# Moving the scale of phi(K) onto V, converting score tiles in pairs, and building the identity's ramp in PSUM, in a gated mix of linear and softmax attention

## The chip, the core and the metric

The kernel runs on one core of a Trainium2 chip. The time is what the device takes for one execution, in microseconds; the median of three runs stands for a kernel. Five engines work side by side, each on its own list of instructions in order: PE (matrix products into PSUM), ACT (activation functions such as exp), DVE (elementwise work and reductions), POOL (elementwise work on SBUF) and SP, which here only issues transfers. They wait for each other through semaphores. PSUM has eight banks of 512 fp32 words in each of 128 partitions.

## The reference

Two attention layers over the same x (2048 rows, 512 columns, 32 heads of 16), mixed by a gate; the inputs are bf16. A is linear attention with a softmax feature map, B is softmax attention.

```
g = sigmoid((x * gate_w).sum(-1))
# A
q, k, v = split(x @ A_wqkv)                       # 32 heads of 16
phi(t)  = concat[softmax(t @ w_phi), softmax(-(t @ w_phi))]    # 32 features a head
kv = einsum("bhsf,bhsd->bhfd", phi(k), v);  z = sum over s of phi(k)
a  = (phi(q) @ kv) / (phi(q) @ z + 1e-6)  @ A_wo
# B
b  = softmax(q k^T / 4) v @ B_wo                  # 2048 x 2048 scores for each head
out = g * a + (1 - g) * b
```

## The kernel before

**Softmax attention is the bulk.** The scores are cut into 2048 tiles of 128 keys x 512 queries: 32 blocks (a chunk of 512 queries, and one of the heads of each group of four), each with 4 heads x 16 key tiles. A tile is named (b, i, kt). The scores of one tile are one matrix product (`qk_mm`, L819) into one PSUM bank. Its exponential can be made in two ways:

- **By ACT.** Two tiles at a time fill two banks and one `activation` of 1024 columns writes their exponentials (`add_exp`, L898 to L901). Such a pair is a slot; slots alternate between the banks S0, S1 and S2, S3. The exponentials go to a ring of 12 places (`Ebuf`), and `add_pv` multiplies them by V (`pv_mm`, L917 to L922; four heads stand side by side in the columns of PE and add into the one bank psO).
- **By DVE and POOL.** DVE turns one tile of scores into int16 words whose bits, read as bf16, approximate the exponential (`tensor_scalar`, L889). POOL then adds two constants to the words of a group of up to four tiles (`shifted`, L864 to L871, one `int64_add` for each constant), which gives the same values with shifted mantissas, and PE multiplies all three versions by V (`add_pvd`). `DN` (L31) says how many tiles of each of the 32 blocks go this way. They sum to 684 before and 694 after; the other tiles, two by two, make 682 slots before and 677 after.

Scores for DVE, and all the other products of the program, share three banks: psM and the fifth and sixth bank of psS (`MISC`, L503). `fill` (L584) gives a product such a bank, `drain` (L606) is the instruction that empties it and sets it free.

**Linear attention fills the gaps.** For each of 16 row tiles `st`, `phi(1, ...)` (L1161) projects x by a weight that already holds w_phi; ACT takes exp of it and of its negative (`both`, L1169) into `EA`, which has two places; DVE sums each head's 16 features (L1177). For every second tile DVE inverts the sums (L1193) and multiplies the features by them (`scaled`, L1203) into `phiK`. `va_fill` (L1154) projects V, and DVE copies it to `vA`, with a column of ones beside each group of four heads. After eight row tiles `kv_half` (L1217) multiplies `phiK` by `vA`: 128 features (two signs x four heads x 16) by 65 columns, summed over the eight tiles; `kfinal` masks the result to the blocks on the diagonal. Then the same is done for Q (`phi(0, ...)`), whose features go through DRAM to be transposed (`q_write`, `q_turn`), multiplied by K's result (`q_rest`, L1265), and again through DRAM (`o_turn`).

**The start.** The first 512 rows of x come in as they lie (transfers of L513) and PE transposes them by means of an identity matrix. DVE builds the identity (L549 to L553): a ramp 0..31 in every partition by doubling (one memset, five additions), its 32x32 transpose `quad`, and four comparisons of the two. From `quad` come `pmask` and `half2`, masks for even and odd heads. Meanwhile PE runs seven products to warm up (L540), POOL clears tiles and issues a few transfers. The first projections and the first scores follow the transposes of x.

**The order of all work** is made by a planner in the kernel's source (`Plan.layout`, L161): it simulates the engines with assumed durations and at each step takes the ready operation with the lowest priority number. The numbers at the top of the file (L31 to L68) are priorities, paces and paddings of this plan. `K_AT + K_PACE * st` and `Q_AT + Q_PACE * i` are the priorities of the row tiles of K and Q, `KG_AT` to `QG_PACE` the slot from which they may begin, `OP_AT` and `O_AT` those of the output projections, `D_FIRST` the slot after which VectorE tiles begin. The engines then run their lists in that fixed order. On PE the scores of the slots come first, and when nothing is ready it multiplies zeros (`zero_mm`, L910 to L912). The flag `lock` marks DVE operations that the plan doesn't put beside one of POOL.

Four output tiles end the program. Two of them (`SPLIT`) are made in two parts, the larger one beforehand (`out_part`, L1102, evicted at L1107), and two by `out_last` (L1111, evicted by ACT at L1119).

Of the kernel before, what the change touches and what calls it, by code (L numbers as in the profile page):

```python
# [9 lines left out]
F32 = mybir.dt.float32  # L10
# [20 lines left out]
DN = (8, 20, 18, 22, 26, 22, 22, 20, 20, 18, 20, 18, 22, 22, 22, 22, 22, 22, 22, 26, 26, 20, 22, 26, 18, 26, 24, 18, 18, 20, 32, 20)  # L31
# [4 lines left out]
STICK = 56.1  # L36
UNITS = 564.8
W_AT = 21.402
D_FIRST = 14
# [6 lines left out]
T_PRIO = 31.922  # L46
DQ_PRIO, DQ_K = 6.035, 1.527
KG_AT, KG_PACE, QG_AT, QG_PACE = 48.282, 10.47, 269.933, 10.468
R1_AT, R1_PACE, R2_AT, R2_PACE, R3_AT, R3_PACE = 34.139, 13.552, 132.978, 16.57, 282.947, 5.294
TR_LAT, TR_ISSUE = 3.0, 0.4  # L50
OP_AT, OP_PACE = 686.29, 4.0
SPLIT = (14, 15)
O_AT, O_PACE = 514.821, 11.487
# [3 lines left out]
QK_TOL = (0.374, 0.192)  # L57
TURN_PAD = 2.257
G_DEEP = 6
K_AT, K_PACE, Q_AT, Q_PACE = 74.787, 10.55, 262.62, 10.076  # L60
POOL_ADDS = (0, 203, 69, 203, 69, 203, 69, 195, 69, 235, 69, 203, 69, 195, 69, 202, 69, 218, 69, 203, 101, 203, 68, 195, 69, 219, 65, 203, 71, 203, 69, 203)
SHIFT = (0.25, 3.63, -8.78, -3.32, -9.03, -1.63, -2.79, 0.92, 2.51, 6.48, 3.43, 8.42, 1.31, -1.12, -3.56, -1.52, 5.83, 8.06, 0.55, 2.18, 3.47, 1.77, 2.23, -4.16, -0.22, 0.96, 4.59, -6.01, -4.6, -0.62, -4.99, 2.66)
P64, W64 = 0.19, 0.21
M_LATE = -15.682
D_AHEAD = 23.328
CONT = -58.411
# [12 lines left out]
class Op:  # L79
    __slots__ = ("eng", "dur", "prio", "fn", "deps", "succ", "nd", "ready", "end", "lat", "sem", "count",  # L80
                 "name", "full", "extra", "room", "fill", "bank_of", "acq", "rel", "seq", "clock", "take", "pos", "margin", "done", "kind", "heads", "lock", "cols", "alive", "semval", "pad")

    def __init__(self, eng, dur, prio, fn, name):
# [10 lines left out]
        self.pad = 0.0  # L94
        self.kind, self.heads, self.lock = None, (), False
# [13 lines left out]
class Bank:  # L109
    def __init__(self, name, ap):  # L110
        self.name, self.ap = name, ap
        self.free, self.shared = True, True
        self.last, self.until = [], 0.0


class Plan:
# [43 lines left out]

    def layout(self):  # L161
        for op in self.ops:
            op.nd = len(op.deps)
            for d in op.deps:
                d.succ.append(op)
# [15 lines left out]
        while left:  # L181
# [30 lines left out]
            for e in ENGINES:  # L212
# [11 lines left out]
                if e == "pe" and last_pe is not None and busy[e] > t - 1e-6:  # L224
                    want = {"qk": "dq", "dq": "dq"}.get(last_pe, "term")
                    for item in sorted(queues[e]):
                        o = item[2]
                        if o.kind == want and not used_heads & set(o.heads) and o.ready <= pe_start + RIDE_TOL and (
                                o.kind == "dq" or o.prio < T_PRIO or active >= ACTIVE[3]):
                            if o.acq is not None:  # L230
# [4 lines left out]
                                o.acq.bank = min(bs, key=lambda b: max([0.0] + [x.end for x in b.last]))  # L235
# [21 lines left out]
                while queues[e] and pick is None:  # L257
# [5 lines left out]
                    elif op.lock and max(lock_end[o] for o in lock_end if o != e) > t + 1e-9:  # L263
                        pass
                    elif op.take is not None:
                        if all(b.free for b in op.take):
                            pick = op
                    elif op.acq is not None:
                        bs = [b for b in op.acq.banks if b.free and b.shared and b.until <= t + 1e-9]
                        if bs:  # L270
                            op.acq.bank = min(bs, key=lambda b: max([0.0] + [o.end for o in b.last]))
                            pick = op
# [29 lines left out]
                op = pick  # L302
                if e == "pe":
# [43 lines left out]
                heapq.heappush(finish, (op.end, op.seq, 1, op))  # L347
                heapq.heappush(events, op.end)
# [5 lines left out]
    def emit(self, block, sems):  # L354
        counts = {e: 0 for e in ENGINES}
# [71 lines left out]
def _build(ctx, nc, A_x, A_wqkv, A_w_phi, A_wo, B_wqkv, B_wo, gate_w, out):  # L427
# [22 lines left out]
    vAf = sb([128, NT * 8 * 65], name="vA")  # L450
    vA = vAf[:].rearrange("p (a b c) -> p a b c", a=NT, b=8)
# [22 lines left out]
    kv_sb = sb([128, 8, 65], F32, name="kv")  # L474
# [4 lines left out]
    ramp = sb([128, 32], name="ramp")  # L479
    quad = sb([128, 32], name="quad")  # L480
    half2 = sb([128, 2], name="half")
    mask64 = sb([128, 64], name="mask64")
# [9 lines left out]
    psS = ctx.enter_context(nc.psum_tensor("psS", [128, 3072], F32))  # L492
    psO = ctx.enter_context(nc.psum_tensor("psO", [128, 512], F32))
    psM = ctx.enter_context(nc.psum_tensor("psM", [128, 512], F32))
    bS = [Bank(f"S{i}", psS[:, 512 * i:512 * (i + 1)]) for i in range(6)]
    bO = Bank("O", psO[:])
    bM = Bank("M", psM[:])
# [39 lines left out]
    def warm_fn(e):  # L537
        ins = None
        for _ in range(7):
            ins = e.matmul(psM[:], lhsT=Ebuf[:, 0, 0:128], rhs=Ebuf[:, 0, 0:512], start=True, stop=True)  # L540
        return ins
# [6 lines left out]
    small = lambda fn, reads, writes, name, prio=-9.5: P.add("dve", 0.16, prio, fn, reads=reads, writes=writes, name=name)  # L548
    small(lambda e: e.memset(ramp[:, 0:1], 0.0), (), ["ramp"], "r0")  # L549
    for n in (1, 2, 4, 8, 16):  # L550
        small(lambda e, n=n: e.tensor_single_scalar(ramp[:, n:2 * n], ramp[:, 0:n], float(n), ALU.add), ["ramp"], ["ramp"], f"r{n}")  # L551
    small(lambda e: e.transpose(quad[:], ramp[:]), ["ramp"], ["quad"], "quad")
    P.join_writes([small(lambda e, q=q: e.tensor_tensor(ident[32 * q:32 * q + 32, 32 * q:32 * q + 32], ramp[32 * q:32 * q + 32, :],  # L553
                                                        quad[32 * q:32 * q + 32, :], ALU.is_equal), ["ramp", "quad", "id"], [], f"id{q}")
                   for q in range(4)], "ident")
    P.join_writes([small(lambda e, n=n: e.tensor_scalar(pmask[:, n:n + 1], quad[:, 0:1], 16.0, QSCALE, op0=(ALU.is_lt, ALU.is_ge)[n],
                                                        op1=ALU.mult), ["quad"], [], f"pm{n}", -9) for n in range(2)], "pmask")
    P.join_writes([small(lambda e, n=n: e.tensor_single_scalar(half2[:, n:n + 1], quad[:, 0:1], 16.0, (ALU.is_lt, ALU.is_ge)[n]), ["quad"], [],
                         f"hh{n}", 0.0) for n in range(2)], "half2")
# [14 lines left out]
    pool(0.4, -3, lambda e: e.memset(vA[:, :, :, 64:65], 1.0), writes=["vA1"], name="vA1")  # L574
# [248 lines left out]
    def add_qk(j):  # L823
# [15 lines left out]
        op.kind, op.heads = "qk", [t[1] for t in ts]  # L839
        if j < 2:  # L840
            op.margin = 0.1
# [35 lines left out]
    def add_group(g):  # L877
        ft, ops, tb = opening(g["t"]), [], bufs[g["t"]][0]
        before = list(dq_ops)
        dq_ops.clear()  # L880
# [560 lines left out]
```

## Time and profile before

| | us |
|---|---|
| median of 3 runs (lowest to highest) | 704.83 (704.63 to 707.05) |
| the profiled execution | 704.55 |
| its span, first to last instruction | 702.5 |
| first exponential of the softmax starts | 13.79 |
| last one ends | 691.56 |

The groups of DVE and POOL that the change touches (line, engine, operation, tiles and shapes, count; busy us, mean ns of one; idle time before and who ended it):

```profile
L1203 DVE TENSOR_TENSOR phiK_t<-EA_t,stat_t 128x1024 bf16<-128x1024 bf16 x16 | 19.9, 1244 | 0.1
L1177 DVE TENSOR_REDUCE stat_t<-EA_t 128x64 f32<-128x1024 bf16 x16 | 19.4, 1210 | 2.3 <-ACT EA_t L1171 2.2
L1193 DVE RECIPROCAL stat_t<-stat_t 128x128 f32<-128x128 f32 x8 | 7.6, 944 | 0.0
L1158 DVE CAST vA_t<-psS 128x512 bf16<-128x512 f32 x11 | 7.5, 683 | 0.0
L551 DVE TENSOR_SCALAR ramp_t<-ramp_t 128x4 bf16<-128x4 bf16 x1 | 5.1, 5143 | 0.0
L1158 DVE CAST vA_t<-psM 128x512 bf16<-128x512 f32 x5 | 3.4, 683 | 0.0
```

Busy times of the engines by stretch (start:end, length, then busy us and count of PE, weight loads, DVE, ACT, POOL; the granted PE clock, the share of DMA, GB/s):

```profile
13.79:50.00 36.21, 35.49 (x385) 13.14 (x384) 23.36 (x40) 35.81 (x39) 9.96 (x13) 1.00 0.41 97
50.00:260.00 210.00, 207.62 (x2139) 64.79 (x2137) 189.44 (x296) 207.09 (x236) 105.99 (x109) 1.00 0.07 16
260.00:460.00 200.00, 195.06 (x2057) 59.90 (x2055) 190.19 (x312) 198.06 (x225) 112.91 (x117) 1.00 0.14 36
460.00:691.60 231.60, 227.22 (x2383) 67.58 (x2376) 205.17 (x383) 227.18 (x252) 127.69 (x130) 0.99 0.26 62
```

A duration is that of one instruction from start to end; instructions of one engine overlap a little, so the step from one start to the next can be shorter. A matrix product's busy time is modelled, and products that stand side by side in PE count each.

### The profile page before, as it was taken

What the parts mean: (1) busy time and instruction counts of PE and PEld (TensorE: products, weight loads), DVE (VectorE), ACT (ScalarE), POOL (GpSimd) and SP (SyncE); (2) the same over time, 40 slices, a digit from 0 to 9 for tenths busy, and PEclk for the clock granted to TensorE, in tenths of its full rate; (3) what the DMA queues carried; (4) which work ended last, traced back from release to release, by engine and by line L of the source; (5) the groups of instructions that cost most, each with busy time, mean ns of one, the idle gap of its engine ahead of it and who ended that gap; (6) DMA issues with size and microseconds to landing.
All of it is one profiled execution on the core that took longest, in us unless ns stands there. A gap on an engine that the chain in (4) does not pass through costs nothing.

```text
span 702.5 us, 17206 instructions
## 1 busy us (share of the span) xinstructions
PE 683.7 (97%) x7083; PEld 214.1 (30%) x7083; DVE 623.3 (89%) x1056; ACT 672.1 (96%) x753; POOL 369.3 (53%) x394
## 2 busy tenths in 40 slices
PE   6999999999999999999999999999999999999999
PEld 3332332333322332233222222332223322332333
DVE  6499879999999699999999999999989999997783
ACT  3999999999999999999999999999999999999994
POOL 7056457555454155553665665645556554455453
PEclk9999999999999999999999999999999999999999
DMA  6600101001000000000013023121321133125121
GB/s 132 161 19 10 26 17 25 11 13 22 10 17 10 9 21 7 26 10 12 20 29 93 10 75 80 27 65 58 70 70 28 43 80 70 48 84 92 49 62 38
DMA packets 67454, 30.72 MB, mean 44 GB/s; under 512 B 52696, under 2 KB 62296, under 8 KB 67376
## 3 DMA queue, kind: packets, MB, share of 16 engines
q1 hardware_dynamic: 66368, 28.95, 17.2%
q8 instruction: 56, 0.92, 0.6%
q10 hardware_dynamic: 576, 0.52, 0.2%
q0 software_dynamic: 432, 0.15, 0.2%
q14 instruction: 22, 0.18, 0.1%
HBM read 7.87 MB, written 8.88 MB: 24 GB/s over the span
## 4 chain that ended last, share of the span: by engine, by line
PE 76%; ACT 17%; DVE 6%; issue 1%
PE psO L922 28%; PE psS L819 25%; ACT E_t L901 16%; PE psS L614 8%; PE psM L614 6%; PE psO L912 4%; ACT EA_t L1171 1%; DVE ramp_t L551 1%; PE psM L819 1%; DVE Tx_t L889 1%; PE psM L684 1%; PE psS L671 1%; DVE Ty_t L889 1%; DVE statq_t L1177 0%; DVE Tf_t L1016 0%
## 5 line engine op out<-in xcount | busy, mean ns | idle before, releaser
L901 ACT ACTIVATE E_t<-psS 128x1024 bf16<-128x1024 f32 x682 | 642.6, 1062 | 11.0 <-PE psS L819 6.0
L819 PE MATMUL psS<-qz_t,kTB_t 32*128 32x512 bf16 x1829 | 275.5, 385 | 9.5 <-ACT E_t L901 7.7
L819 PEld LDWEIGHTS psS<-qz_t,kTB_t 32*128 32x128 bf16 x1829 | 70.0, 91 | 249.1 <-ACT E_t L901 179.7
L889 DVE TENSOR_SCALAR Tx_t<-psS 128x512 int16<-128x512 f32 x181 | 120.6, 681 | 8.6 <-PE psS L819 4.2
L922 PE MATMUL psO<-E_t,vaug_t 128*32 128x512 bf16 x1364 | 113.8, 388 | 0.0
L871 POOL INT64_ADD vA_t<-vA_t x68 | 67.4, 996 | 45.5 <-PE psO L922 28.6
L819 PE MATMUL psM<-qz_t,kTB_t 32*128 32x512 bf16 x219 | 84.3, 385 | 0.0
L871 POOL INT64_ADD Ty_t<-Tx_t x28 | 28.3, 1009 | 54.8 <-DVE Tx_t L889 43.1
L889 DVE TENSOR_SCALAR Ty_t<-psS 128x512 int16<-128x512 f32 x74 | 50.1, 683 | 6.5 <-PE psM L819 3.1
L889 DVE TENSOR_SCALAR Tx_t<-psM 128x512 int16<-128x512 f32 x71 | 48.4, 681 | 4.4 <-PE psS L819 2.9
L871 POOL INT64_ADD Ty_t<-Ty_t x39 | 39.3, 1007 | 17.0 <-PE psO L922 10.6
L922 PE MATMUL psO<-vA_t,vaug_t 128*32 128x512 bf16 x486 | 46.8, 383 | 0.0
L912 PE MATMUL psO<-xT_t,zero_t 128*32 128x512 bf16 x484 | 44.5, 386 | 0.0
L922 PE MATMUL psO<-Ty_t,vaug_t 128*32 128x512 bf16 (+1 forms) x406 | 41.8, 384 | 0.0
L922 PEld LDWEIGHTS psO<-E_t,vaug_t 128*32 128x32 bf16 x1364 | 23.9, 95 | 43.6 <-issue 40.8
L889 DVE TENSOR_SCALAR Ty_t<-psM 128x512 int16<-128x512 f32 x48 | 32.7, 682 | 1.6 <-PE psM L819 1.2
L889 DVE TENSOR_SCALAR oT_t<-psS 128x512 int16<-128x512 f32 x45 | 30.1, 683 | 4.4 <-PE psS L819 3.8
L889 DVE TENSOR_SCALAR Tz_t<-psS 128x512 int16<-128x512 f32 x44 | 29.3, 680 | 2.7 <-PE psS L819 2.6
L889 DVE TENSOR_SCALAR WAT_t<-psS 128x512 int16<-128x512 f32 x43 | 28.8, 679 | 2.8 <-PE psM L819 2.2
L871 POOL INT64_ADD WoA_t<-WoA_t x17 | 16.8, 989 | 26.9 <-PE psO L922 25.2
L871 POOL INT64_ADD phiQT_t<-Tx_t x17 | 16.0, 940 | 27.4 <-DVE Tx_t L889 27.4
L889 DVE TENSOR_SCALAR vA_t<-psS 128x512 int16<-128x512 f32 x42 | 28.3, 679 | 1.0 <-PE psS L819 0.8
(205 smaller groups left out, 1041.7 us busy)
## 6 DMA issues: line engine op xcount, KB each, us to landing
dpq<-EA_t SPq DMA_DIRECT2D x16, 256.0 KB, 2.2
Rb_t<-lr SPq DMA_DIRECT2D x120, 32.0 KB, 1.8
dpo<-kv_t SPq DMA_DIRECT2D x16, 128.0 KB, 1.7
qz_t<-qz_t SPq DMA_DIRECT2D x120, 16.0 KB, 1.8
Tf_t<-Tf_t SPq DMA_DIRECT2D x60, 32.0 KB, 2.0
WB_t<-in_B_wqkv_dram SPq DMA_DIRECT2D x3, 384.0 KB, 4.6
out_dram<-WvA_t SPq DMA_DIRECT2D x8, 128.0 KB, 1.8
out_dram<-WB_t SPq DMA_DIRECT2D x6, 128.0 KB, 1.7
```

The lines of the kernel that those rows point to most:

```text
L551: small(lambda e, n=n: e.tensor_single_scalar(ramp[:, n:2 * n], ramp[:, 0:n], float(n), ALU.add), ["ramp"], ["ramp"], f"r{n}")
L614: return [lambda e, ap, i=i: e.matmul(ap, lhsT=lhs[i], rhs=rhs[i], start=(i == 0), stop=(i == len(lhs) - 1)) for i in range(len(lhs))]
L671: mms = [lambda e, ap, i=i, t=t: e.matmul(ap[:, 128 * i:128 * (i + 1)], lhsT=xT[:, t, NQ * c + 128 * i:NQ * c + 128 * (i + 1)], rhs=W_B[:, ...
L684: mms = [lambda e, ap, i=i, t=t: e.matmul(ap[:, 256 * i:256 * (i + 1)], lhsT=xT[:, t, NQ * c + 128 * (2 * hf + i):NQ * c + 128 * (2 * hf + ...
L819: return e.matmul(bank, lhsT=kT_B[32 * i:32 * i + 32, ROW[b // 2] % 2, 128 * kt:128 * (kt + 1)], rhs=qz[32 * i:32 * i + 32, b // 2 % 4, b ...
L871: op = P.add("pool", P64 + W64 * size, d_prio(g["ts"][0]) - 5.0 + (0.0 if key == "s" else M_LATE), lambda e: e.int64_add(words(dst), words ...
L889: ops.append(drain(f, mm, "dve", 0.70, d_prio(d), lambda e, ap, q=q: e.tensor_scalar(quarter(tb, q).bitcast(I16), ap, EXPB, 0.0, op0=ALU.a ...
L901: op = P.add("act", 0.051 + 0.4267 * n, 0.0, lambda e: e.activation(Ebuf[:, j // 2 % EPAIRS, 512 * SZ[0] * (j % 2):512 * SZ[0] * (j % 2) + ...
L912: ins = e.matmul((psO if bank is None else bank)[32 * i:32 * i + 32, :], lhsT=zero[:], rhs=xT[:, 0, 0:NQ], start=bank is not None, stop=ba ...
L922: return e.matmul(psO[32 * i:32 * i + w, :], lhsT=vaug[:, kt, o:o + w], rhs=rhs, start=start, stop=stop, tile_position=(0, 32 * i), skip_g ...
L1171: ins = e.activation(EA[:, b, :].rearrange("p (g s c) -> p s g c", s=2, c=64)[:, sgn, :, :], ap.rearrange("p (g c) -> p g c", c=64), ACTF. ...
```

## The change

- **Scale of phi(K).** `scaled` is gone: ACT writes the exponentials of K straight into `phiK` and they stay as they are. The reciprocal sums multiply V instead. For each row tile, V is projected after the sums are known and evicted twice, once for each sign, by a DVE product with the sums broadcast over 16 columns; POOL copies the reciprocal sums themselves beside V, where the ones stood. `vA` holds 8 row tiles, two signs each, instead of 16 tiles. The product of `kv_half` is then two products of 64 features (one for each sign) that stand side by side in PE's columns, with 68 columns.
- **Pairs.** psM becomes the seventh bank of psS, so that the three shared banks lie in a row. Where two tiles of the same group are ready for DVE (or one is to be within `PAIR_WAIT`) and lie in neighbouring banks in the same order as in the group, the planner makes one `tensor_scalar` of 2 x 512 columns of them; both banks are freed when it ends. `choose` picks banks so that the order fits.
- **Identity.** The ramp lies in the first columns of psS, in fp32; `quad`, its transpose, in SBUF in fp32; a second transpose, `column`, in PSUM, serves the masks.
- **Numbers.** `DN`, and most of the priorities, paces and paddings of the plan, have other values; `QK_PAD`, `D1_PAIR` and `PAIR_WAIT` are new.

```
-DN = (8, 20, 18, 22, 26, 22, 22, 20, 20, 18, 20, 18, 22, 22, 22, 22, 22, 22, 22, 26, 26, 20, 22, 26, 18, 26, 24, 18, 18, 20, 32, 20)
+DN = (6, 20, 18, 20, 26, 22, 22, 20, 22, 18, 20, 18, 22, 20, 22, 22, 26, 22, 22, 28, 26, 22, 22, 28, 16, 24, 24, 18, 22, 22, 32, 22)
-STICK = 56.1
+STICK = 15.702
-D_FIRST = 14
+D_FIRST = 26
-KG_AT, KG_PACE, QG_AT, QG_PACE = 48.282, 10.47, 269.933, 10.468
+KG_AT, KG_PACE, QG_AT, QG_PACE = 23.892, 7.205, 270.949, 12.608
-OP_AT, OP_PACE = 686.29, 4.0
+OP_AT, OP_PACE = 641.917, 4.0
-K_AT, K_PACE, Q_AT, Q_PACE = 74.787, 10.55, 262.62, 10.076
+K_AT, K_PACE, Q_AT, Q_PACE = 73.65, 11.18, 262.327, 12.484
...
+    def mates(self, a, b):
+        return b.kind == "D1" and a.half[0] == b.half[0] and abs(a.rel.bank.index - b.rel.bank.index) == 1 and (
+            a.half[1] - b.half[1]) * (a.rel.bank.index - b.rel.bank.index) > 0
...
+                    elif op.kind == "D1" and any(r <= t + PAIR_WAIT and self.mates(op, x) for r, _, x in pending["dve"]):
+                        pass
...
+                        op.fn = lambda e, wide=wide, a=(min(q, q2), max(q, q2)), b=(min(b, b2), max(b, b2)): wide(e, a, b)
+                        op.dur = D1_PAIR
+                        op.deps = op.deps + [d for d in other.deps if d not in op.deps]
+                        op.rel = [op.rel.bank, other.rel.bank]
...
+            return e.tensor_scalar(dst[:, a[0]:a[1] + 1:a[1] - a[0], :].bitcast(I16), src[:, b[0]:b[1] + 1:b[1] - b[0], :], EXPB, 0.0,
+                                   op0=ALU.add, op1=ALU.max)
...
-    psM = ctx.enter_context(nc.psum_tensor("psM", [128, 512], F32))
+    psM = psS[:, 3072:3584]
...
-    ramp = sb([128, 32], name="ramp")
-    quad = sb([128, 32], name="quad")
+    quad = sb([128, 32], F32, name="quad")
+    ramp, column = psS[:, 0:32], psS[:, 32:64]
...
-    def va_fill(st, prio):
+    def va_fill(st, prio, after):
...
+        for s in range(2):
+            drain(f, mm, "dve", 0.70, prio, lambda e, ap, s=s: e.tensor_tensor(
+                vA[:, m, :, s, 0:64].rearrange("p g (j d) -> p g j d", j=4), ap.rearrange("p (g j d) -> p g j d", g=8, j=4),
+                by[:, :, s, :].unsqueeze(3).to_broadcast([128, 8, 4, DH]), ALU.mult),
+                reads=[("rs", b), ("ss", b)], writes=[("vA", m, s)], name=f"VAe{st}.{s}", last=s == 1)
+        P.add("pool", 0.3, prio, lambda e: e.tensor_copy(vA[:, m, :, :, 64:68], by), reads=[("rs", b), ("ss", b)],
+              writes=[("vA", m, 2)], name=f"VAr{st}")
...
-    def scaled(qk, st, e3, dst, dkey, prio):
-        b = st % 2
-        phi_ops.append(P.add("dve", 1.22, prio, lambda e: e.tensor_tensor(
-            dst.rearrange("p (g f) -> p g f", f=DH), e3, stat[:, b, :].unsqueeze(2).to_broadcast([128, 64, DH]), ALU.mult),
-            reads=[("EA", b), ("rs", b), ("ss", b)], writes=[dkey], name=f"phi{qk}.{st}"))
-        phi_ops[-1].lock = True
...
+                        for s in range(2):
+                            ins = e.matmul(ap[64 * s:64 * s + 64, 68 * gg:68 * gg + 68], lhsT=phiK[:, m, 128 * g + 64 * s:128 * g + 64 * s + 64],
+                                           rhs=vA[:, m, g, s, :], start=(m == 0), stop=(m == 7), tile_position=(0, 64 * s))
```

159 lines of the change are left out of this document (97 added, 62 removed).

## The prediction

> **What bounds the kernel now.** I read four views. First the page, for the engine that is full.
>
> ```profile
> span 702.5 us, 17206 instructions
> PE 683.7 (97%) x7083; PEld 214.1 (30%) x7083; DVE 623.3 (89%) x1056; ACT 672.1 (96%) x753; POOL 369.3 (53%) x394
> ...
> L901 ACT ACTIVATE E_t<-psS 128x1024 bf16<-128x1024 f32 x682 | 642.6, 1062 | 11.0 <-PE psS L819 6.0
> ```
>
> ACT is 96% busy, nearly all of it the 682 softmax exponentials of L901. PE shows 97%, but 596 of its matmuls (L912) are zero products that only fill gaps, so PE is not the limit. Second, the sums over the stretches around the stream of exponentials (columns: PE, PEld, DVE, ACT, POOL busy):
>
> ```profile
> 0.00:13.79 13.79, 8.05 (x45) 4.58 (x46) 10.20 (x22) 2.59 (x5) 12.75 (x27) 1.00 0.69 140
> ...
> 691.60:702.50 10.90, 10.21 (x93) 4.08 (x91) 4.90 (x8) 1.37 (x2) 0.00 (x0) 1.00 0.15 50
> ```
>
> The span is a start of 13.8 us, a stream of 677.8 us and a tail of 10.9 us. In the stream ACT is busy 668.1 us, so only 9.7 us there are lost. The time falls if exponentials go away, if the stream begins earlier, or if the tail shrinks; it rises if something behind ACT makes it wait. Third, the start in order of time:
>
> ```profile
> 1.18 3.17 PE L540 MATMUL psM<-E_t 128*128 128x512 bf16 x7 [1.18 <-DVE ramp_t L549]
> 1.18 6.62 DVE L551 TENSOR_SCALAR ramp_t<-ramp_t 128x1 bf16<-128x1 bf16 x5
> 2.43 2.29 POOL L562 MEMSET vaug_t<- 128x512 bf16 x1
> 4.86 1.40 POOL L564 MEMSET qz_t<- 128x1536 bf16 x1
> 7.84 0.21 DVE L552 STREAM_TRANSPOSE quad_t<-ramp_t 128x32 bf16<-128x32 bf16 x1
> 8.09 0.76 DVE L553 TENSOR_TENSOR ident_t<-ramp_t,quad_t 32x32 bf16<-32x32 bf16 x4
> 8.90 0.61 PE L1295 MATMUL psO<-ident_t,phiK_t 128*128 128x128 bf16 x4 [4.55 <-DVE ident_t L553]
> ...
> 13.79 12.02 ACT L901 ACTIVATE E_t<-psS 128x1024 bf16<-128x1024 f32 x13 [1.38 <-PE psS L819]
> ```
>
> Five tiny additions that build the ramp last 6.62 us, one of them 5.14 us alone, while POOL clears tiles; the others take 0.16 to 0.67. The identity is done at 8.85, and PE had waited 4.55 us for it: this chain sets when the first exponential starts. Fourth, the end:
>
> ```profile
> 690.54 1.02 ACT L901 ACTIVATE E_t<-psS 128x1024 bf16<-128x1024 f32 x1 [0.49 <-PE psS L819]
> 690.75 1.04 PE L614 MATMUL psM<-WoA_t,phiK_t 128*128 128x512 bf16 x4
> ...
> 692.37 0.10 PEld L922 LDWEIGHTS psO<-E_t,vaug_t 128*32 128x32 bf16 x2 [0.42 <-issue]
> ...
> 696.82 1.03 PE L614 MATMUL psM<-WoA_t,phiK_t 128*128 128x512 bf16 x4
> ```
>
> The last exponential ends at 691.56, but its P.V product starts at 692.37, behind seven matmuls of an output part, and the last output tile is still being multiplied at 698.7.
>
> **The change, part by part.**
>
> **Ten more VectorE tiles.** The sum of DN goes from 684 to 694, so 2048-694 = 1354 tiles stay with ACT: 677 exponentials instead of 682. One costs 642.6/682 = 0.942 us; in unbroken rows (13 in 12.02, 5 in 4.93) the step is 0.92 to 0.98. 5 x 0.942 = **-4.7** (-4.6 to -4.9). Each tile moved gives DVE one conversion (step 0.60 us: starts at 302.40 and 303.00), 10 x 0.60 = +6.0 on DVE; POOL gets 184 groups instead of 182, 2 x 2 additions x 1.0 = +4 of its 333 idle; PE gets two more P.V passes per tile, four side by side in 0.215 us, so 20/4 x 0.215 = +1.1, in place of zero products (52.4 us).
>
> **The ramp in PSUM.** Nothing in this trace writes PSUM from DVE. The nearest small rows are 0.15 us (L1134, 128x4 read from PSUM) and, for the same additions not stretched much, 0.16 to 0.31. One memset, five additions, two transposes and four comparisons at 0.15 to 0.31 are 1.8 to 3.7; I take 0.20 each, 2.4, since the comparisons already step at 0.19. From 1.08 the identity is done at about 3.5 (2.9 to 4.8). What is late next: the warm-up matmuls end at 4.35, and the four pieces of x land 2.8 to 3.3 after issue at 0.73 and 1.2, so by 4.5. The transposes then start at 4.5 instead of 8.90. The query projection, at 10.62 now, would come at 6.2; its weights, issued by POOL at 1.30, land 4.4 later, at 5.7 (6.8 if counted from the end of the issue, then 0.6 is lost). Other bound: the copies of x (PSUM to SBUF, 0.42 us) would now meet POOL's clearing of qz, until 6.26; held back until then, they lose 1.2. That they run at 0.42 beside POOL's DMA issues now (9.16 to 13.3) speaks against it. The column for the masks adds a transpose of 0.2 after the identity, beside PE's transposes. Value **-4.4**; with all three losses (0.3 for a late identity, 0.6, 1.2) -2.3, and up to -4.9 if the first products, 0.31 each after PE's idle time, run at the 0.22 that the same shape takes in L671 later; 0 if the stall stays.
>
> The Trainium skill (SBUF — State Buffer, "SBUF: two separate sides") says that VectorE and GpSimd share one port pair as an exclusive lock, taken by VectorE only in a mode that needs two SBUF ports. By it an addition with its operands in PSUM would never wait and the gain is whole. The trace agrees with the wait, but the 5.14 us span three clearings, where one instruction's wait would be at most 2.29.
>
> **K's scale moved to V.** Off DVE: 16 products of L1203 at a step of 1.13 (303.00 to 304.13), -18.1, and 16 evictions of L1158 at 0.59, -9.4. On DVE: 32 evictions that multiply by a broadcast. No row is the same; bounds are the plain eviction, 0.59, and L1076's product from PSUM, 1.41/2 = 0.70. I take 0.65: +20.8. POOL adds 16 small copies (L579, 128x64, 0.24): +4. Since nothing in the stream waits for L1203 except POOL (9.1 us in all), the direct effect on the span is **0**; DVE gets 6.7 us lighter, which pays for the ten tiles. The added wait: V's product takes a shared bank after the sums and holds it through the reciprocal (0.94) and two evictions, about 2.2 us instead of 0.7. Behind it on PE's queue stand conversions' score products and the exponentials' own.
>
> On PE, K.V becomes 256 matmuls of 64 columns instead of 128 of 128. The old ones step at 3.4/64 = 0.053 us. Side by side they cost nothing, one after the other +128 x 0.053 = 6.8; the P.V rows do run four narrow products side by side (8 in 0.62 us), so I take +1. It is covered by zero products, 23.7 us between 50 and 460 us; without cover it costs up to 6.8.
>
> The Trainium skill (TensorEngine Tiling (Array Packing), "Key Properties") says that changing the tiling mode drains TensorE; the trace shows it as weight loads coming after 0.42 us instead of 0.21 to 0.23. 32 pieces of K.V with a change on each side would make 32 x 2 x 0.2 = 12.8 us of PE, an estimate; this rule speaks against the change and gives a rival below.
>
> **Pairs.** Two conversions of 0.60 become one. 4 elements take 0.15 us and 512 take 0.68, so 1024 take 0.68 + 0.53 = 1.21, a step of 1.13: 0.07 saved per pair. Zero to 347 pairs; they need neighbouring banks filled at once, and perhaps a third of the tiles find that: 115 x 0.07 = 8 us off DVE. Price: the first bank of a pair stays taken 0.53 longer, and only three banks are shared.
>
> **The retuned numbers** move whole phases: output parts due at 642 instead of 686, Q's pace slower (12.5 for 10.1), block 0's VectorE tiles start after exponential 26 instead of 14. In the tail the seven matmuls ahead of the last P.V cost 692.37-691.56 = 0.8, and both parts together hold PE 14 x 0.215 = 3.0 us. If they get ahead of the last exponentials, up to 2.5 is gained; but they wait for transposes issued at 678.7 to 683.8, which follow VectorE work that yields to conversions, so a later Q could lose as much. I take **-1.0** (+1.5 to -2.5).
>
> **Sum.** 702.5-4.4-4.7-1.0 = 692.4. The profiled execution took 704.55, 2.05 around its span, and the median is 0.28 above it: 692.4 + 2.05 + 0.28 = **694.7 us**.
>
> **Rivals.**
> *More than that*: lighter DVE also removes a quarter of the 9.7 us that ACT loses in the stream, 2.4, and the tail gives 2.5. 694.7-2.4-1.5 = 690.8. For it: DVE runs back to back for tens of us. Against: ACT's waits are for PE.
> *The start gives nothing*: another stall takes the ramp's place (POOL against the copies of x, or weights that land late). Tail unchanged too: 704.8-4.7 = 700.1. For it: loads were never tested at 5 us earlier. Against: they are issued by 2.1 us.
> *K.V in narrow tiles is not covered*: 694.7 + 6.8 = 701.5. For it: after a change of shape weight loads come 0.2 us later. Against: the cover of 23.7.
> *Shared banks run out* (the other side): pairs hold 115 x 0.53 = 61 bank-us more, V's products 16 x 1.5 = 24; together 85. A score product waiting for a bank blocks the exponentials' behind it on PE. If a fifth reaches ACT, 17 us: 694.7 + 17 = 711.7. It turns slower above 10.1/85 = 12%. For it: three banks, PE in order. Against: PE's waits for DVE are now at most 0.6 us in any group of the stream.
> That the change does not do what it says is covered by the second.
>
> **Chances.** Forecast 0.62 (its own range 691.5 to 698), more 0.12, no start 0.13, narrow tiles 0.04, banks 0.09. A measurement here tells 0.5%, 3.5 us, from no change: the line is 701.3 and 708.4. Faster: 0.62 + 0.12 + 0.09 of the third = 0.83; same 0.04 + 0.04 = 0.08; slower 0.09. Range 690 to 702: it takes in the start's bounds and the third and fourth cases, and leaves out the banks and part of "more".
>
> **What would show it.** Right: first L901 at 9 to 10 us, 677 of them, ramp additions all below 0.35, the stream's ACT idle 8 to 12 us, P.V of the last exponential within 0.5 us. Wrong: ACT idle in the stream over 15 us with waits on score products behind DVE (banks), or a first exponential after 11 us.

## The result, and the profile after

| | before | after |
|---|---|---|
| median in the same session (lowest to highest) | 705.94 (704.63 to 707.23) | 715.45 (713.78 to 715.82) |
| ratio, 95% interval | | 1.013 (1.0101 to 1.016) |
| span of the profiled execution | 702.5 | 713.9 |
| start: up to the first exponential | 13.79 | 8.27 |
| stream: first to last exponential | 677.8 | 688.8 |
| tail: from the last exponential's end | 10.9 | 16.9 |

The changed kernel is 1.3% slower. The forecast was 694.7 us with a range of 690 to 702, and had faster at 0.83. The start gave 5.5 us, the stream took 11.0 and the tail 6.0: -5.5 + 11.0 + 6.0 = +11.4 to within rounding, the whole difference of the spans (the medians differ by 9.5).

The page of the changed kernel: the span, the engines, and the group of exponentials (busy us, mean ns | idle time before, and who ended it).

```profile
span 713.9 us, 17723 instructions
PE 696.1 (98%) x7355; PEld 218.3 (31%) x7355; DVE 615.2 (86%) x1012; ACT 671.8 (94%) x748; POOL 376.8 (53%) x413
```

```profile
L953 ACT ACTIVATE E_t<-psS 128x1024 bf16<-128x1024 f32 x677 | 641.5, 1051 | 21.8 <-PE psS L862 15.5 <-PE psO L974 1.4
```

The busy times over start, stream and tail (start:end, length, then busy us and count of PE, weight loads, DVE, ACT, POOL; PE clock, DMA share, GB/s):

```profile
0.00:8.27 8.27, 6.81 (x45) 3.91 (x46) 4.66 (x23) 2.52 (x4) 7.36 (x14) 1.00 0.75 159
8.27:697.03 688.76, 674.56 (x7191) 208.61 (x7191) 604.35 (x981) 667.94 (x742) 367.82 (x398) 0.99 0.17 42
697.03:713.90 16.87, 14.69 (x123) 5.78 (x121) 6.22 (x10) 1.38 (x3) 1.65 (x2) 1.00 0.15 48
```

There are five exponentials fewer, and yet ACT is busy for 667.9 us of the stream, against 668.1 before. The reason is in the step from one exponential's start to the next: 0.904 us in an unbroken row, but over 1.02 when one has to start alone, because neighbours then no longer overlap. Added up over all pairs of neighbouring exponentials with no other work of ACT between them, what lies above 0.904 is 30.4 us before and 45.7 after. Five exponentials at 0.904 are -4.5 us; the breaks add 15.3; the sum is 10.8, about the 11.0 of the stream. So the stream is longer because its row of exponentials is broken more often and for longer, not because there is more work.

Who breaks it, in the views of waits of ACT and then of PE (waiting, waited for: us in total, times, longest):

```profile
ACT E_t L953 <- PE psS L862: 15.5, 46, 2.7
```

```profile
PE psS L862 <- ACT E_t L953: 4.6, 15, 0.6
PE psS L657 <- ACT phiK_t L1231: 1.2, 2, 0.6
PE psS L581 <- DVE psS L592: 1.2, 1, 1.2
PE psS L1321 <- DVE WAT_t L939: 0.7, 2, 0.4
```

ACT waits 46 times for scores (before: 6.0 us in 16 waits). PE itself hardly waits for DVE: such groups are 0.7 us at most once the stream runs, and all of them together 6.6 us (before: 2.7; in e11 below, the fastest version, 8.5). PE makes the scores late because of what stands ahead of them in its own list. The longest wait shows how. A part of PE's list between 463 and 477 us (start, duration):

```profile
467.39 0.39 PE L862 MATMUL psS<-qz_t,kTB_t 32*128 32x512 bf16 x2 [0.40 <-ACT E_t L953]
467.80 0.30 PE L1321 MATMUL psS<-kzbd_t,WAT_t 128*128 128x68 bf16 x4
...
469.00 0.63 PE L657 MATMUL psS<-Wp_t,xT_t 128*128 128x512 bf16 x2 [0.30 <-DVE Tx_t L939]
...
473.13 1.90 PE L974 MATMUL psO<-E_t,vaug_t 128*32 128x512 bf16 x16
474.82 1.07 PE L974 MATMUL psO<-vA_t,vaug_t 128*32 128x512 bf16 x8
475.67 0.64 PE L974 MATMUL psO<-Ty_t,vaug_t 128*32 128x512 bf16 x4
476.10 0.47 PE L974 MATMUL psO<-WB_t,vaug_t 128*32 128x512 bf16 x4
476.50 0.40 PE L862 MATMUL psS<-qz_t,kTB_t 32*128 32x512 bf16 x4
```

Two blocks of queries change places here. The old block's sums leave psO by a copy (L1068, 0.68 us) that DVE makes at 467.66, behind a row of other DVE work; no P.V product runs from 464.05 to 471.7. The bank is free at 468.34, but scores and projections (L657) stand ahead of the first P.V products in PE's list. Two of these run at 471.71, and from 473.13 on 32 run in one go, ahead of the next scores at 476.50. ACT starts its next exponential at 476.93, after a wait of 2.67 us. That PE needs 3.4 us for these 32 has a second cause, in the sums over the same time:

```profile
466.03:469.45 3.42, 2.40 (x17) 0.72 (x14) 3.42 (x7) 3.42 (x5) 0.07 (x1) 1.00 0.21 71
469.45:472.86 3.41, 3.41 (x17) 0.88 (x16) 2.02 (x6) 3.24 (x5) 0.00 (x0) 0.50 0.38 125
472.86:476.27 3.41, 3.41 (x35) 1.09 (x32) 2.47 (x5) 1.41 (x2) 0.27 (x1) 0.50 0.09 22
```

After 3.4 us in which PE was busy for only 2.40, its granted clock is 0.50, just when the backlog has to be worked off. In the whole trace the clock is halved for 17.1 us of the stream, in three places (6.83 at 469, 3.41 at 558, 6.83 at 681); before, for 3.41 us in one. (That is one execution of each; how much the clock of the kernel before differs from one execution to the next stands under the experiments.)

The tail, in DVE's and POOL's lists before and after:

```profile
684.94 1.29 DVE L889 TENSOR_SCALAR vA_t<-psS 128x512 int16<-128x512 f32 x2 [0.67 <-PE psS L819]
692.48 0.75 DVE L1107 TENSOR_SCALAR xT_t<-psM,gT_t 128x512 f32<-128x512 f32 x1 [6.24 <-PE psM L614]
```

```profile
693.17 1.23 DVE L929 TENSOR_SCALAR Tx_t<-psS 128x1024 int16<-128x1024 f32 x1 [0.96 <-PE psS L862]
...
701.77 0.71 DVE L1094 STREAM_TRANSPOSE Tf_t<-psO 128x512 f32<-128x512 f32 x1
```

```profile
696.05 0.61 POOL L915 INT64_ADD Ty_t<-Tx_t  x1
698.69 0.61 POOL L915 INT64_ADD Ty_t<-Ty_t  x1 [2.02 <-PE psO L974]
699.35 1.04 POOL L915 INT64_ADD Wp_t<-Wp_t  x1
```

Before, the last VectorE tile is converted by 686.2, five us ahead of the last exponential's end at 691.56, and its additions and products are done when ACT is. After, the last group is converted at 694.4, between the exponentials, and its second POOL additions run until 700.4, when ACT has been done for 3.4 us. The last P.V products (to 701.6) need them, and the chain from `Tf` to the output follows. But these additions are not all of the tail. PE has no gap from the last exponential's end to its last output product; the sums over that stretch, before and after:

```profile
691.56:698.71 7.15, 7.15 (x46) 2.86 (x43) 4.90 (x8) 0.69 (x2) 0.00 (x0) 1.00 0.08 25
```

```profile
697.03:708.62 11.59, 11.59 (x75) 4.64 (x77) 6.22 (x10) 0.69 (x2) 1.65 (x2) 1.00 0.14 48
```

So 4.4 of the 6.0 us are PE's, which has more left to multiply: 43 products of the output against 28, and 26 of P.V against 12. The other 1.5 us come behind it: the last transfer lands 3.9 us after its issue, before 1.7. No run shows why; in e4 below, with the same order, it is 1.7 again.

### The profile page after: what moved, and what is told of

Read it like the earlier page. It is cut to its first block, busy times and chain, and to the rows that moved or that the text cites. A ratio compares the mean times of both kernels' runs of the same rounds, so it can differ in the third digit from the quotient of the medians.

```text
span 713.9 us, 17723 instructions
## 1 busy us (share of the span) xinstructions
PE 696.1 (98%) x7355; PEld 218.3 (31%) x7355; DVE 615.2 (86%) x1012; ACT 671.8 (94%) x748; POOL 376.8 (53%) x413
## 3 DMA queue, kind: packets, MB, share of 16 engines
q1 hardware_dynamic: 66368, 28.95, 16.9%
## 4 chain that ended last, share of the span: by engine, by line
PE 77%; ACT 11%; DVE 10%; issue 2%; ACTq 0%
PE psO L974 28%; PE psS L862 25%; PE psS L657 14%; ACT E_t L953 10%; PE psO L964 5%; DVE Tx_t L939 2%; DVE WAT_t L939 1%; PE psS L727 1%; DVE Ty_t L939 1%; PE psS L714 1%; DVE Tf_t L1068 1%; DVE vA_t L939 1%; DVE Wp_t L939 1%; ACT phiK_t L1231 1%; PE psS L1321 1%
## 5 line engine op out<-in xcount | busy, mean ns | idle before, releaser
L862 PE MATMUL psS<-qz_t,kTB_t 32*128 32x512 bf16 x2048 | 282.4, 387 | 6.5 <-ACT E_t L953 4.6
L939 DVE TENSOR_SCALAR Tx_t<-psS 128x512 int16<-128x512 f32 x214 | 141.3, 681 | 10.5 <-PE psS L862 10.2
L939 DVE TENSOR_SCALAR Ty_t<-psS 128x512 int16<-128x512 f32 x108 | 72.3, 683 | 7.4 <-PE psS L862 7.0
L964 PE MATMUL psO<-xT_t,zero_t 128*32 128x512 bf16 x636 | 58.2, 385 | 0.0
L915 POOL INT64_ADD Ty_t<-Ty_t x39 | 39.6, 1016 | 24.9 <-PE psO L974 20.8
L939 DVE TENSOR_SCALAR Wp_t<-psS 128x512 int16<-128x512 f32 x58 | 38.4, 681 | 5.1 <-PE psS L862 4.7
L657 PE MATMUL psS<-Wp_t,xT_t 128*128 128x512 bf16 x128 | 41.3, 389 | 1.0 <-DVE Wp_t L939 0.4
L974 PE MATMUL psO<-Ty_t,vaug_t 128*32 128x512 bf16 x410 | 41.9, 385 | 0.0
L939 DVE TENSOR_SCALAR oT_t<-psS 128x512 int16<-128x512 f32 x58 | 38.6, 681 | 3.4 <-PE psS L862 2.9
L657 PE MATMUL psS<-xT_t,WB_t 128*128 128x512 bf16 x116 | 36.0, 385 | 1.2 <-ACT phiK_t L1231 0.6
L929 DVE TENSOR_SCALAR Tx_t<-psS 128x1024 int16<-128x1024 f32 x21 | 25.7, 1221 | 6.8 <-PE psS L862 6.6
```

What stands on the lines that cost most here:

```text
L657: return [lambda e, ap, i=i: e.matmul(ap, lhsT=lhs[i], rhs=rhs[i], start=(i == 0), stop=(i == len(lhs) - 1)) for i in range(len(lhs))]
L862: return e.matmul(bank, lhsT=kT_B[32 * i:32 * i + 32, ROW[b // 2] % 2, 128 * kt:128 * (kt + 1)], rhs=qz[32 * i:32 * i + 32, b // 2 % 4, b ...
L915: op = P.add("pool", P64 + W64 * size, d_prio(g["ts"][0]) - 5.0 + (0.0 if key == "s" else M_LATE), lambda e: e.int64_add(words(dst), words ...
L929: return e.tensor_scalar(dst[:, a[0]:a[1] + 1:a[1] - a[0], :].bitcast(I16), src[:, b[0]:b[1] + 1:b[1] - b[0], :], EXPB, 0.0, op0=ALU.add, ...
L939: ops.append(drain(f, mm, "dve", 0.70, d_prio(d), lambda e, ap, q=q: e.tensor_scalar(quarter(tb, q).bitcast(I16), ap, EXPB, 0.0, op0=ALU.a ...
L964: ins = e.matmul((psO if bank is None else bank)[32 * i:32 * i + 32, :], lhsT=zero[:], rhs=xT[:, 0, 0:NQ], start=bank is not None, stop=ba ...
```

## The experiments

Two theories stood at the outset. *Order*: the loss lies in the order of work that the planner makes of the new numbers, so each part is harmless by itself. *Parts*: the pairs' hold on the shared banks (my fourth rival), or the narrow K.V products, cost the time directly. Runs of the kernel before spread from 704.3 to 710.0 us in these sessions, and the mean granted clock goes with it (0.998 in all runs up to 705.3 us, 0.983 in those from 709.7 us), so ratios to it are given with their intervals. The *reckoned end* is the end of the order as `Plan.layout` itself simulates it with its assumed durations; it is no time on the chip.

**e1, the ramp alone.** The kernel before with the ramp, `quad` and `column` as in the change; the planner keeps its order.

```
-    ramp = sb([128, 32], name="ramp")
-    quad = sb([128, 32], name="quad")
+    quad = sb([128, 32], F32, name="quad")
+    ramp, column = psS[:, 0:32], psS[:, 32:64]
```

> The kernel before with one part of the change: the ramp, its transpose and the masks in PSUM; every engine's list keeps its order apart from the one added transpose. If the start's stall was the ramp's wait alone, the first exponential starts at 8.2 to 8.6 us instead of 13.8 and the whole 5.3 us reaches the end: 699 to 701 us. If the gain of the start is taken back later (a load, or an order that fits the late start), 703 to 705.

702.12 us, ratio 0.9916 (0.988 to 0.9952). The first exponential starts at 8.49 instead of 13.79. This part gains by itself, in the old order: 4.9 us by the medians of that session (707.02 before). It is less than the whole 5.3 that I expected to reach the end: in the profiled executions the stream is 3.0 us longer than before, and its clock is halved for 10.2 us instead of 3.41.

**e2, the changed kernel with each pair made as two conversions**, in the pair's place. The order is the same, and both banks are freed when the second is done.

```
-            return e.tensor_scalar(dst[:, a[0]:a[1] + 1:a[1] - a[0], :].bitcast(I16), src[:, b[0]:b[1] + 1:b[1] - b[0], :], EXPB, 0.0,
-                                   op0=ALU.add, op1=ALU.max)
+            for x, y in zip(a, b):
+                ins = e.tensor_scalar(dst[:, x, :].bitcast(I16), src[:, y, :], EXPB, 0.0, op0=ALU.add, op1=ALU.max)
+            return ins
```

> The changed kernel with each pair written as two conversions of 512 columns one behind the other, in the same place of the list and with the same waits. If the loss lies in the order of the work that the new numbers make, the 55 pairs matter little: 0 to +4 us against the changed kernel (55 x 0.07), 715 to 719 us. If wide conversions themselves cost (a bank held longer, DVE slower on two banks), it is faster: 705 to 712.

716.58 us, ratio 1.0116 (1.0077 to 1.0154), no different from the changed kernel. The wide instruction is not the cost. The banks are held as long here, so this run says nothing of the hold; e7 does.

**e3, K.V with whole tiles.** One product of 128 features in place of two of 64 side by side. Both signs take the first sign's V, so that part of linear attention is not computed as the reference has it.

```
-                        for s in range(2):
-                            ins = e.matmul(ap[64 * s:64 * s + 64, 68 * gg:68 * gg + 68], lhsT=phiK[:, m, 128 * g + 64 * s:128 * g + 64 * s + 64],
-                                           rhs=vA[:, m, g, s, :], start=(m == 0), stop=(m == 7), tile_position=(0, 64 * s))
-                        return ins
+                        return e.matmul(ap[:, 68 * gg:68 * gg + 68], lhsT=phiK[:, m, 128 * g:128 * g + 128],
+                                        rhs=vA[:, m, g, 0, :], start=(m == 0), stop=(m == 7))
```

> The changed kernel with K.V as one product of 128 feature columns instead of two of 64 side by side; both signs then take the first sign's V, so the output differs. If narrow tiles cost TensorE's drain at each change of shape, 3 to 7 us less than the changed kernel: 708 to 712. If they lie beside other work, within 1 us of it: 714 to 716.

713.95 us, ratio 1.0089 (1.0055 to 1.0123). The medians differ by 1.5 us with overlapping intervals. In the profiled executions the stream, in which all products of K.V lie, is 688.4 us instead of 688.8; the rest of the difference is in the tail, where there are none. So the narrow tiles cost about 0.4 us in the stream, which is not clear of noise, and not the 3 to 7 of the drain.

**e4, PE kept busy.** The scores of 24 slots, ahead of the three stretches with a halved clock, are multiplied twice; the order is the same.

```
-            for m, t in enumerate(ts):
-                ins = qk_mm(e, t, psS[:, 512 * (base + m):512 * (base + m + 1)])
+            for _ in range(2 if any(k <= j < k + 8 for k in (453, 536, 658)) else 1):
+                for m, t in enumerate(ts):
+                    ins = qk_mm(e, t, psS[:, 512 * (base + m):512 * (base + m + 1)])
```

> The changed kernel with the score products of 24 slots (8 each around 466, 555 and 678 us) issued twice into the same banks, to keep TensorE occupied where the granted clock fell to half in its trace (for 6.8, 3.4 and 6.8 us); nothing else moves. If the halved clock is the cause of the late losses, clock 0.995 or more and 6 to 10 us less: 705 to 709 us. If the clock falls only because the other engines hold TensorE up, the time stays within 2 us of 715, whatever the clock does.

711.12 us, ratio 1.0066 (1.0035 to 1.0096). More work makes it 4.3 us shorter, less than the 6 to 10 that I expected. The halved clock goes from 17.1 us to 3.41. The sums over the stretch of the long wait, here:

```profile
466.03:469.45 3.42, 2.85 (x25) 0.75 (x25) 3.40 (x7) 3.21 (x5) 0.00 (x0) 1.00 0.16 51
469.45:472.86 3.41, 3.41 (x34) 1.14 (x36) 2.88 (x8) 3.40 (x5) 0.00 (x0) 1.00 0.38 125
472.86:476.27 3.41, 3.25 (x50) 1.25 (x43) 3.38 (x8) 3.12 (x4) 2.45 (x3) 1.00 0.08 22
```

PE is busy for 2.85 us instead of 2.40, the clock stays whole, and ACT is busy for 3.12 us in the last row instead of 1.41. But ACT still waits 13.5 us for scores, in 47 waits. In the profiled executions 3.3 us are gained in the stream and 1.6 in the tail, behind PE's last product, where the last transfer lands earlier. One of e4's ten runs had a clock of 0.988, the changed kernel's, and took 716.35 us. So the clock is an aggravation worth some 3 to 4 us, and the waits are there without it.

**e5, another order of the same work.** e1 with one number more, 0.08 us added to the time that the planner reckons for scores to become readable; no instruction of the computation differs.

```
-QK_PAD = 0.0
+QK_PAD = 0.08
```

> The kernel before with the ramp in PSUM (as in the ramp run, 702.1 us) and with nothing else but 0.08 us added to the time that the scheduler reckons for a score product to be readable (QK_PAD). No instruction of the computation is changed, added or removed; only the order of the streams (and the number of zero products that fill gaps of TensorE) comes out otherwise, and by the scheduler's own reckoning it ends 12.2 us later. Order theory: the reckoned idle time of ScalarE appears on the chip, +8 to +14 us over the ramp run, 710 to 716 us. Parts theory (the loss sits in the pairs' banks, the narrow K.V products or the V scale): none of these is here, so 701 to 704 us.

721.22 us, ratio 1.0185 (1.0131 to 1.0239); 19 us above e1 and slower than the changed kernel, with none of its parts but the ramp. ACT's waits in this run:

```profile
ACT E_t L907 <- PE psS L824: 14.0, 38, 2.0
ACT E_t L907 <- PE psM L824: 3.2, 8, 1.4
ACT E_t L907 <- PE psO L928: 2.4, 3, 1.1
```

The same picture as in the changed kernel, made by order alone. The loss was larger than the 8 to 14 expected: the planner reckons 12.2, the chip makes 19 of it.

**e6, e7, e8: the parts with numbers of their own.** For each set of parts, on top of e1, the planner's numbers were searched for an early reckoned end. e6 has the V scale, without pairs; e7 has the pairs (33 of them), without the V scale; e8 has all three parts; none has `QK_PAD`. Of e6's numbers, against those of the kernel before:

```
-STICK = 56.1
+STICK = 283.151
-D_FIRST = 14
+D_FIRST = 23
-KG_AT, KG_PACE, QG_AT, QG_PACE = 48.282, 10.47, 269.933, 10.468
+KG_AT, KG_PACE, QG_AT, QG_PACE = (6.2, 13.545, 269.537, 9.649)
...
-M_LATE = -15.682
+M_LATE = -221.055
```

> The kernel before with the ramp in PSUM and the scale of phi(K) moved onto V (with the narrow products of K.V and the POOL copies of the sums), without the pairs and without QK_PAD, with 681 exponentials on ScalarE, and with scheduling numbers of its own, for which the scheduler reckons an end 0.2 us from that of the kernel before. Order theory: about the ramp run's time, 699 to 705 us, so faster than before, since the part itself costs nothing. Parts theory: the narrow products and the second eviction of each V tile cost 6 us or more on the chip, 708 to 714 us.

> The kernel before with the ramp in PSUM and the pairs (33 of them in this order), without the V scale and without QK_PAD, 682 exponentials, with scheduling numbers of its own, for which the reckoned end is 2.2 us after that of the kernel before. Order theory: 701 to 707 us. Parts theory, if the pairs cost by holding shared banks longer: 709 to 715 us.

> All three parts of the change, but QK_PAD at 0 and other scheduling numbers (683 exponentials, 25 pairs), for which the reckoned end is 8.8 us after that of the kernel before, about where the changed kernel's own lies (8.1 us after). Order theory: the reckoned end decides, so this lands near the changed kernel, 708 to 716 us, although its numbers are others. If instead QK_PAD or the particular numbers of the changed kernel cost something that the reckoning doesn't see, it comes out at 700 to 706 us.

e6: 701.6 us, 0.9926 (0.9901 to 0.9951). e7: 703.82 us, 0.9953 (0.9929 to 0.9976). e8: 714.32 us, 1.0089 (1.006 to 1.0119). Neither the V scale nor the pairs make it slower than the kernel before in an order made for them (e7 with 33 pairs, not the changed kernel's 55); all three parts in an order with a late reckoned end land near the changed kernel, with other numbers than its own.

**e9, fewer VectorE tiles in the last block.** The changed kernel with 18 there instead of 22, so 679 exponentials; the order is the same up to exponential 671.

```
-DN = (6, 20, 18, 20, 26, 22, 22, 20, 22, 18, 20, 18, 22, 20, 22, 22, 26, 22, 22, 28, 26, 22, 22, 28, 16, 24, 24, 18, 22, 22, 32, 22)
+DN = (6, 20, 18, 20, 26, 22, 22, 20, 22, 18, 20, 18, 22, 20, 22, 22, 26, 22, 22, 28, 26, 22, 22, 28, 16, 24, 24, 18, 22, 22, 32, 18)
-UNITS = 564.8
+UNITS = 566.4685376661743
```

> The changed kernel with 18 instead of 22 VectorE tiles in the last block: 690 VectorE tiles, 679 exponentials; UNITS is scaled so that the due times of everything else stay, and the scheduler's order is the same up to exponential 671. Sum theory (an exponential fewer is 0.94 us less, as in my prediction): two more exponentials make it 1.9 us longer, 716 to 718 us. Order theory: the last exponential ends about 2 us later and the tail is about 2 us shorter, since VectorE and GpSimd are late with the last group and not ScalarE: no change beyond 1 us, 714 to 716 us.

714.21 us, ratio 1.0112 (1.0074 to 1.0151): no change. The last exponential ends 2.0 us later, and the tail is 2.1 us shorter:

```profile
699.06:713.80 14.74, 12.67 (x103) 5.12 (x98) 5.46 (x9) 1.38 (x3) 0.61 (x1) 1.00 0.16 54
```

PE's last output product ends at 708.8, in the changed kernel at 708.6. At the end, the two exponentials that the tiles had saved bought nothing.

**e10 and e11, 677 and 682 exponentials.** Both as e6, with numbers searched anew: e10 with the changed kernel's 677 exponentials (the sum of `DN` 694), e11 with 682. Of e10's numbers, against those of e6:

```
-DN = (8, 20, 18, 22, 26, 22, 22, 20, 22, 18, 18, 18, 22, 22, 24, 22, 22, 22, 22, 26, 28, 20, 22, 26, 18, 26, 24, 18, 18, 20, 30, 20)
+DN = (8, 20, 18, 22, 24, 22, 24, 20, 22, 18, 18, 18, 22, 22, 24, 22, 24, 22, 22, 26, 26, 20, 22, 30, 18, 26, 24, 18, 18, 20, 34, 20)
```

> As the run with the V scale, the ramp and its own numbers (681 exponentials, 701.6 us), but with the changed kernel's count of 677 exponentials and 694 VectorE tiles, and scheduling numbers found for that; no pairs, no QK_PAD. The scheduler reckons the last exponential 2.5 us earlier and the end 1.6 us later than for that run. Sum theory: 4 x 0.94 us are saved, 697 to 699 us. Order theory: the reckoned end decides, 702 to 705 us, with a tail of 14 to 16 us.

> The kernel before with the ramp in PSUM and the V scale, 682 exponentials as before, no pairs, no QK_PAD, and scheduling numbers for which the reckoned end is 1.1 us before that of the kernel before with the ramp. Order theory: a little under the ramp run's 702.1 us, 698 to 702 us, the best of the versions here. If the V scale's own work costs more on the chip than is reckoned: 704 us or more.

e10: 704.22 us, 0.9959 (0.9935 to 0.9982). With four exponentials fewer than e6 it is 2.6 us longer, not 3.8 shorter: its last exponential ends at 688.72 (e6: 687.65) and its tail is 14.3 us (e6: 10.4); the planner had reckoned the last exponential 2.5 us earlier than e6's. e11: 698.42 us, 0.9887 (0.9857 to 0.9917), faster than both kernels. Its page:

```profile
span 697.2 us, 17537 instructions
PE 670.1 (96%) x7204; PEld 215.3 (31%) x7267; DVE 610.5 (88%) x1057; ACT 672.9 (97%) x753; POOL 371.6 (53%) x409
```

```profile
L906 ACT ACTIVATE E_t<-psS 128x1024 bf16<-128x1024 f32 x682 | 643.4, 1056 | 11.3 <-PE psS L823 4.3 <-PE psM L823 2.6
```

ACT's idle time ahead of exponentials is half of the changed kernel's, with five exponentials more. It gains mainly by the ramp; e1's interval and e11's overlap, so the V scale's own gain isn't shown.

All orders with the ramp in PSUM together, by reckoned end (e2, e3 and e4 have the changed kernel's):

| run | parts beside the ramp | exponentials | reckoned end | median |
|---|---|---|---|---|
| e11 | V scale | 682 | 679.3 | 698.42 |
| e1 | none | 682 | 680.2 | 702.12 |
| e6 | V scale | 681 | 680.4 | 701.60 |
| e10 | V scale | 677 | 682.0 | 704.22 |
| e7 | pairs | 682 | 682.4 | 703.82 |
| the changed kernel | V scale, pairs | 677 | 688.3 | 715.45 |
| e9 | V scale, pairs | 679 | 688.6 | 714.21 |
| e8 | V scale, pairs | 683 | 689.0 | 714.32 |
| e5 | none | 682 | 692.4 | 721.22 |

A straight line through the nine, 1.64 us on the chip for 1 us reckoned, leaves at most 1.2 us for any of them (e2 and e4 would lie 2.3 above and 3.1 below it). Given the reckoned end, neither the parts nor the number of exponentials is needed to tell the time. Three of the four late orders have all three parts, though; e5 alone shows a late one without them. The kernel before has e1's order and so its reckoned end, 680.2: the planner itself puts the changed kernel 8.1 us later, which could have been worked out from the two sources before any run. Why the slope is above one is only partly shown: late scores leave PE thin, and the clock is halved after that (in e5 for 20.5 us).

## Why the prediction was wrong

- **The step that failed is "the retuned numbers, -1.0 (+1.5 to -2.5)".** I priced them in the tail alone and let the stream's 9.7 us of lost ACT time stand. But these numbers remake the order of every engine's list. In the stream ACT's idle time became 688.8 - 667.9 = 20.8 us, and the tail grew by 6.0 where I had it shrink by 1.0. e5 shows that one such number, with no part but the ramp, costs 19 us; the table shows that the changed kernel's time is the one that its order lets one expect. That the order is late is shown; whether the new numbers alone or the parts that they have to fit make it late is not (see below).
- **"Ten more VectorE tiles, -4.7" fell too.** The five exponentials are gone, but ACT's busy time in the stream is the same within 0.2 us, since each break in the row costs overlap. e10 (four fewer, 2.6 us longer) shows it with other numbers, e9 (two more, no change) in the changed kernel. The sum per exponential holds only while nothing but ACT sets the end, and in the tail PE's row without a gap sets it.
- **The start was right in its mechanism and mis-sized: -5.5 for -4.4.** The five additions take 1.00 us together and the identity is done at 3.34 (I had 3.5):

```profile
1.22 1.00 DVE L594 TENSOR_SCALAR psS<-psS 128x1 f32<-128x1 f32 x5
2.43 2.30 POOL L606 MEMSET vaug_t<- 128x512 bf16 x1
2.50 0.84 DVE L596 TENSOR_TENSOR ident_t<-psS,quad_t 32x32 bf16<-32x32 f32 x4
6.00 0.60 PE L740 MATMUL psS<-xT_t,WB_t 128*128 128x256 bf16 x4 [0.28 <-DVE xT_t L1357]
8.27 1.02 ACT L953 ACTIVATE E_t<-psS 128x1024 bf16<-128x1024 f32 x1 [0.99 <-PE psS L862]
```

  The query projection starts at 6.00 (forecast 6.2); from there to the first exponential it is 2.27 us, where I kept the old 13.79 - 10.62 = 3.17. None of the three losses came. The Trainium skill (SBUF — State Buffer, "SBUF: two separate sides") would have an addition between PSUM operands not wait for POOL. The rows agree: the third addition starts at the same time in both kernels, beside the same work of POOL (a transfer that it issues from 1.30 to 2.36), and takes 5.14 us before and 0.17 after. The other additions are done at 2.22, before POOL's clearings begin, so none was tried beside a clearing.

```profile
1.62 5.14 DVE L551 TENSOR_SCALAR ramp_t<-ramp_t 128x4 bf16<-128x4 bf16 x1
```

```profile
1.62 0.17 DVE L594 TENSOR_SCALAR psS<-psS 128x4 f32<-128x4 f32 x1
```

- **K's scale on V, 0: right.** e6 and e11 hold the time of the ramp alone. An eviction with the product takes 0.680 us, a plain one 0.683; DVE is 8.1 us lighter over the span, of which the ramp's additions alone are 5.6.
- **Narrow tiles, covered: right**, about 0.4 us in the stream (e3). The Trainium skill (TensorEngine Tiling (Array Packing), "Key Properties") says that a change of tiling drains TensorE; I had estimated 12.8 us of PE from that. The 0.4 us is all that the stream shows of it; what PE's gaps absorbed isn't shown.
- **Pairs:** the planner found 55, not 115, so some 3.9 us off DVE instead of 8. One takes 1.22 us, as estimated (1.21). e7, with 33 of them, is no slower than its reckoned end lets one expect.
- **The rival "shared banks run out" gave 711.7, near the result, and its signal came** (ACT idle over 15 us), but not its place: PE waits 0.7 us at most for a group of DVE in the stream, 6.6 in all where e11 has 8.5, and e5 has much the same waits of ACT without pairs and V scale. The planner foresees how long a bank is held, so the hold may still act through the order that it makes; no run parts the two. A right number doesn't confirm a mechanism.
- **"P.V of the last exponential within 0.5 us"** was wrong: 0.93, behind eight products of an output part (696.13 to 698.0).

What stays open: which of the new numbers costs most, since any one of them moves the whole order; whether it is the numbers or the parts that make the order late, since they can't be exchanged one for one (laid out by `Plan.layout`, not run, the changed kernel with the old numbers ends at a reckoned 711.6, and e1 with the new ones at 704.4); and whether all three parts together have an order as good as e11's. The search found none below a reckoned 689 for them, which doesn't show that there is none.

## What to carry to other kernels

Where a planner writes the engines' lists, a change of its numbers is a change of everything: price it by the end that the planner itself reckons and by the idle time in the stream, not by the sum of what the parts add and take off, and compare parts only in orders made for each. When one engine is 96% busy and others nearly as full, work taken off the fullest is a gain only if the others can follow; look at what ends the tail before counting it. And a gain that needs no new order (the ramp) is worth measuring alone: here it was some -5 us, and it was buried.

## What was not expected of the hardware

- The PE clock fell to 0.50 with PE never idle for long: in the changed kernel after 3.42 us of which it was busy for 2.40, with gaps of at most 0.40 us. The Trainium skill (TensorE: Matmul & The Clock Gate) gives as the usual cause an idle gap beyond some 3.4 us ("HAM oscillation — how this bites in real kernels"), and as another one frequent short idle times between groups of products ("A second HAM failure mode: psum-queue depth-cycling"). The halved times in the lengths 3.41 and 6.83 us agree with a window of that length, and the rows are of the second kind. In the changed kernel's trace they also begin whole multiples of 3.413 us apart (469.45, then 26 of them later 558.19, then 36 later 681.07). What share of a window must be busy the page doesn't state, and busy time alone doesn't decide it: of two such windows of e11, counted back in steps of 3.413 us from the one halved stretch in its trace (564.21 to 567.62), the first was busy for 2.42 us and the clock stayed whole after it, the second for 3.00, and the clock was halved after it.

```profile
297.97:301.39 3.42, 2.42 (x21) 0.75 (x20) 3.39 (x6) 3.42 (x5) 1.29 (x3) 1.00 0.01 2
560.79:564.21 3.42, 3.00 (x28) 0.88 (x25) 3.42 (x7) 3.42 (x5) 1.61 (x2) 1.00 0.37 126
```

- Work added to PE shortened the kernel by 4.3 us (e4), 3.3 of them in the stream by the profiled executions.
- 0.08 us in an assumed latency moved the time by 19 us (e5), with the same instructions but zero products.
